# Joint attention of a diffusion transformer block: text scores, image gate rows and text V in one 32-column run behind the image scores

## The chip, the cores and the metric

One core of a Trainium2 chip runs the whole kernel in one launch. The metric is device time in microseconds (us) of that core; lower is better. TensorE does the matrix products, VectorE and ScalarE work on what it leaves in PSUM, GpSimd (POOL in the profile) and SyncE (SP) mostly issue transfers.

## The reference

Two streams, image (256 tokens) and text (32 tokens), batch 2, width 1152, all in bfloat16, are modulated, attend jointly and are projected out. With `_layernorm` and `_silu` as usual:

```python
mod_i = (_silu(c) @ wmod_img).reshape(B, 6, 1, D)      # shift, scale, gate: the first three are used
mod_t = (_silu(c) @ wmod_txt).reshape(B, 6, 1, D)
hi = _layernorm(x_img) * (1 + sci) + shi;  ht = _layernorm(x_txt) * (1 + sct) + sht
qkvi = hi @ wqkv_img;  qkvt = ht @ wqkv_txt             # q, k, v of each stream
q, k, v = concat([text, image], axis=1) of each
p = softmax(q @ k.T * D ** -0.5);  a = p @ v
out_i = x_img + gai * (ai @ wo_img);  out_t = x_txt + gat * (at @ wo_txt)
```

## The kernel before

All weights are streamed once through five weight slots of 128 x 9 x 1152; SP's queue issues these loads in program order, and a load into a used slot waits for the last reader of that slot. Instructions wrapped in `pin` keep their program order on their engine. What concerns the change is the stage between the last text projection (`qk_txt(1, w_k_t)`) and the output projections (`out_img`, L680).

**Scores.** For each of four image query tiles I0 to I3 (batch b, tile qi), `scores_img` (L584) makes 128 x 288 scores in PSUM with nine matmuls. `scores_txt` (L592) makes the scores of the 2 x 32 text queries with 18 matmuls in four 32-column groups of the array (`tile_position=(0, r0)`): even and odd feature tiles go to different halves, so the two halves must be added afterwards (`half`, a ScalarE copy at L657 and a VectorE add at L660).

**Softmax.** `soft_max` (L563, row maximum, VectorE), `soft_exp` (L570, exponential with row sum, ScalarE), `soft_div` (L575: reciprocal and multiplication on VectorE, and at L580 a small GpSimd multiplication which writes the 32 text-key columns a second time, to columns 320 to 351 of the row block `pb`, where the third key block is transposed from).

**Gate rows.** `img_gate` calls `mod_rows` (L509): 36 matmuls in four 32-column groups give the image gate's rows; a ScalarE copy (L516) takes them to SBUF, two GpSimd DMAs (L518) write them to DRAM. `img_gate_spread` (L528) reads them back over all 128 partitions as `gb`, which `out_img` multiplies by (L693).

**Text V.** `v_txt(r)` (L490) makes one half of the text values: 9 x 2 matmuls, each with both batches' 64 text tokens as 64 columns, in two column groups. `v_txt_out` subtracts a correction on VectorE.

**Transposes.** `p_transposes(b)` (L603) turns the softmax rows of image b by TensorE: 9 transposes of 128 x 128, three key blocks (`kj`) of three row tiles each, the third row tile being the text's `pbs["t"]`. Only `kj == 2` reads the columns that GpSimd wrote. ScalarE copies them to `pT` (L615), and `attn_pair` (L634) multiplies `pT` by the values.

In this stage TensorE's order is: I0, I1, text scores, gate rows, I2, I3, transposes of batch 0 (nine), text V (both halves), transposes of batch 1 (nine), attention. PSUM tiles come from two rings, `ps_mm` with six buffers and `ps_tr` with two. The GpSimd queue's order in this stage is: `pb` of I0, I1, the two gate-row DMAs, `pb` of the text, of I2, of I3, then the `gb` and `xf` loads.

Of the kernel before, what the change touches and what calls it, by code (L numbers as in the profile page):

```python
# [14 lines left out]
def kernel(  # L15
# [14 lines left out]
    nc = tc.nc  # L30
    bf = mybir.dt.bfloat16
    f32 = mybir.dt.float32
    PSUM = bass.MemoryType.PSUM

    B, NI, D = x_img.shape
    NT = x_txt.shape[1]
    P = 128
    KT = D // P
    NTOK = NI + NT
    NIT = (B * NI) // P  # L40
    TPB = NI // P
    NTT = B * NT
    CH = 384
    NCH = D // CH
    VC = 288
# [7 lines left out]
    work = ctx.enter_context(tc.tile_pool(name="work", bufs=2))  # L53
    small = ctx.enter_context(tc.tile_pool(name="small", bufs=4))
    ps_mm = ctx.enter_context(tc.tile_pool(name="ps_mm", bufs=6, space=PSUM))
    ps_tr = ctx.enter_context(tc.tile_pool(name="ps_tr", bufs=2, space=PSUM))

    pin = tc.keep_in_program_order

    def mm(*a, **k):  # L60
        return pin(nc.tensor.matmul(*a, **k))  # L61

    def tr(*a, **k):
        return pin(nc.tensor.transpose(*a, **k))  # L64
# [19 lines left out]
    def load_w(slot, src, c0, splits=(D,)):  # L84
        t = wtile(slot)
        sv = wview(src, c0)
        o = 0
        for n in splits:
            nc.sync.dma_start(t[:, :, o:o + n], sv[:, :, o:o + n])
            o += n  # L90
        return t
# [36 lines left out]
    ident = const.tile([P, P], bf)  # L128
# [22 lines left out]
    ident2 = const.tile([P, P], bf)  # L151
# [227 lines left out]
    HD = D // 2  # L379
# [3 lines left out]
    rows, cols = {}, {}  # L383
# [13 lines left out]
    hT_t = act.tile([P, KT, NTT], bf)  # L397
# [92 lines left out]
    def v_txt(r):  # L490
        ps = ps_mm.tile([P, VC], f32, tag="mm")
        for kt in range(KT):
            for g in range(2):
                c0 = g * HD + r * VC
                mm(ps[64 * g:64 * g + NTT, :], lhsT=hT_t[:, kt, :], rhs=w_v_t[:, kt, c0:c0 + VC],
                   start=(kt == 0), stop=(kt == KT - 1), tile_position=(0, 64 * g))
        return ps

    def v_txt_out(r, ps):
        pin(nc.vector.tensor_sub(v_t[:, r * VC:(r + 1) * VC], ps[:], svb[:, r * VC:(r + 1) * VC]))  # L500
        if r == 0:
            pin(nc.vector.tensor_sub(v_t[0:NTT, HD:HD + NTT], ps[NTT:P, 0:NTT], svb[NTT:P, 0:NTT]))
# [3 lines left out]
        r0 = 64 * h + NT * b  # L506
        return r0, v_t[r0:r0 + NT, c0:c0 + P]

    def mod_rows(w_blk, si):  # L509
        gps = ps_mm.tile([P, VC], f32, tag="mm")  # L510
        for kt in range(KT):
            for g in range(NGG):
                mm(gps[32 * g:32 * g + 32, :], lhsT=sT32[:, kt, :], rhs=w_blk[:, kt, g * VC:(g + 1) * VC],
                   start=(kt == 0), stop=(kt == KT - 1), tile_position=(0, 32 * g))
        g_sb = work.tile([P, VC], bf, tag="garow")
        pin(nc.scalar.copy(g_sb[:], gps[:]))  # L516
        for b in range(B):
            nc.gpsimd.dma_start(gsc[si, b, :].rearrange("(g j) -> g j", g=NGG), g_sb[b:P:32, :])  # L518
# [3 lines left out]
    xf = act.tile([P, 2, VC], bf)  # L522

    def img_gate():
        mod_rows(w_ga_i, 0)

    def img_gate_spread():
        for b in range(B):  # L528
            pin(nc.gpsimd.dma_start(gb[:, b, :], gsc[0, b, :].partition_broadcast(P)))
        for g in range(2):  # L530
            pin(nc.gpsimd.dma_start(xf[64 * g:64 * g + NTT, :, :],
                                    xt_flat.rearrange("t (r g j) -> g t r j", r=2, g=2)[g]))

    def txt_gate():
        mod_rows(w_ga_t, 1)
        for g in range(2):
            for b in range(B):
                r0 = 64 * g + 32 * b
                nc.gpsimd.dma_start(gbf[r0:r0 + NT, :, :],
                                    gsc[1, b, :].rearrange("(r g j) -> g r j", r=2, g=2)[g].partition_broadcast(NT))  # L540
# [4 lines left out]
    w_ga_i = load_w(0, wmod_img, 2 * D)  # L545
    w_v_t = load_w(1, wqkv_txt, 2 * D)
    w_o_i = load_rows(4, wo_img, 0)
    w_ga_t = load_w(3, wmod_txt, 2 * D)
# [8 lines left out]
    qpos = [[0, P, 2 * P], [NT, NT + P, 0]]  # L557

    pbs = {}
# [3 lines left out]
    def soft_max(key, sps, qn):  # L563
        nmx = small.tile([P, 1], f32, tag="nmx")
        pin(nc.vector.reduce_max(nmx[0:qn, :], sps[0:qn, :], axis=AX.X, negate=True))  # L565
        e = work.tile([P, NTOK], f32, tag="e")
        rs = small.tile([P, 1], f32, tag="rs")
        soft[key] = (sps, qn, nmx, e, rs)

    def soft_exp(key):  # L570
        sps, qn, nmx, e, rs = soft[key]
        pin(nc.scalar.activation(e[0:qn, :], sps[0:qn, :], ACT.Exp, bias=nmx[0:qn, :], scale=1.0,
                                 accum_out=rs[0:qn, :]))

    def soft_div(key):  # L575
        sps, qn, nmx, e, rs = soft[key]
        pin(nc.vector.reciprocal(rs[0:qn, :], rs[0:qn, :]))  # L577
        pb = pb_txt if key == "t" else pb_tiles[key[0] * TPB + key[1]]
        pin(nc.vector.tensor_scalar_mul(pb[0:qn, 0:NTOK], e[0:qn, :], rs[0:qn, :]))
        pin(nc.gpsimd.tensor_scalar(pb[0:qn, NI + 2 * NT:NI + 3 * NT], e[0:qn, NI:NTOK], rs[0:qn, :], 0.0,  # L580
                                     op0=ALU.mult, op1=ALU.add))
        pbs[key] = pb

    def scores_img(b, qi):  # L584
        q0 = qi * P
        sps = ps_mm.tile([P, NTOK], f32, tag="mm")
        for ft in range(KT):
            mm(sps[:], lhsT=qkT[:, ft, b, q0:q0 + P], rhs=qkT[:, KT + ft, b, :],
               start=(ft == 0), stop=(ft == KT - 1))
        return sps  # L590

    def scores_txt():  # L592
        sps = ps_mm.tile([P, NTOK], f32, tag="mm")
        for ft in range(KT):
            for b in range(B):
                r0 = 64 * (ft % 2) + NT * b
                mm(sps[r0:r0 + NT, :], lhsT=qkT[:, ft, b, NI:NTOK], rhs=qkT[:, KT + ft, b, :],
                   start=(ft < 2), stop=(ft >= KT - 2), tile_position=(0, r0))
        return sps

    pTs = {}

    def p_transposes(b):  # L603
        pT = work.tile([P, 3, NTOK], bf, tag="pT")
        tiles = [(range(3), ps_tr)] if b == 0 else [((2,), ps_mm), (range(2), ps_tr)]
        for kjs, pool in tiles:
            pT_ps = pool.tile([P, 8 * P], bf, tag="tr" if pool is ps_tr else "mm", name="pT_ps")
            txt = [(2, pbs["t"], ident2 if b else ident)]
            img = [(qi, pbs[(b, qi)], ident) for qi in range(TPB)]
            for n, kj in enumerate(kjs):  # L610
                for qi, pb, perm in (txt + img if b else img + txt):
                    o = n * NTOK + qpos[b][qi]
                    k0 = kj * P - (NT * b if kj == 2 else 0)
                    tr(pT_ps[:, o:o + P], pb[:, k0:k0 + P], perm[:])
            pin(nc.scalar.copy(pT[:, kjs[0]:kjs[-1] + 1, :],  # L615
                               pT_ps[:, 0:len(kjs) * NTOK].rearrange("p (k n) -> p k n", n=NTOK)))
        pTs[b] = pT

    def attn_keys(tiles, first):
        for b, dt in tiles:  # L620
# [25 lines left out]

    I = [(b, qi) for b in range(B) for qi in range(TPB)]

    sp = {key: scores_img(*key) for key in I[:2]}
    soft_max(I[0], sp[I[0]], P)  # L650
    soft_exp(I[0])
    soft_max(I[1], sp[I[1]], P)
    soft_div(I[0])
    soft_exp(I[1])
    st = scores_txt()
    half = work.tile([NTT, NTOK], f32, tag="half", bufs=1)
    pin(nc.scalar.copy(half[:], st[NTT:P, :]))  # L657
    soft_div(I[1])
    img_gate()
    pin(nc.vector.tensor_add(half[:], st[0:NTT, :], half[:]))  # L660
    soft_max("t", half, NTT)
    soft_exp("t")
    for key in I[2:]:
        sp[key] = scores_img(*key)
    soft_max(I[2], sp[I[2]], P)
    soft_exp(I[2])
    soft_div("t")
    soft_max(I[3], sp[I[3]], P)
    soft_exp(I[3])
    soft_div(I[2])  # L670
    soft_div(I[3])
    p_transposes(0)
    for r in range(2):
        v_txt_out(r, v_txt(r))
    p_transposes(1)
    img_gate_spread()
    for dts in ((0, 5, 1), (6, 2, 7), (3, 8, 4)):
        attn_pair(*[[(b, dt) for dt in dts] for b in range(B)])
# [37 lines left out]
    C3 = (CH, CH, CH)  # L716
    out_img(0, C3)
    out_img(1, C3, between=txt_gate)
    out_img(2, C3)
    out_txt()  # L720
# [31 lines left out]
```

## Time and profile before

| | us |
|---|---|
| median of 4 runs | 118.58 (117.89 to 118.74) |
| the profiled execution, its own time | 118.32 |
| its span, first to last instruction | 116.1 |
| TensorE busy in the span | 111.3 (96%), 1036 matmuls |
| VectorE / ScalarE / GpSimd busy | 72.0 / 44.9 / 12.4 |
| granted TensorE clock | 1.00 of full speed |
| DMA | 41.02 MB, mean 353 GB/s |

In the views of the profile an entry names the source line, the engine and the tiles: `sps` are scores, `gps` gate rows, `ps` here text V, `pT_ps` transposes, `aps` attention. All matmuls carry L61 and all transposes L64, the lines of two helpers. A timeline entry gives the start, the time to the end of the last instruction of the entry, and, in square brackets, the idle time before it with what ended it. Successive matmuls overlap, so their pace is read from starts, not from durations.

### The profile page before, as it was taken

To read this page: it belongs to the slowest core of one execution; us is meant where nothing else is said; L and a number is where in the kernel's file an instruction comes from. 1 tells how busy PE (TensorE), PEld (TensorE's weight loads), DVE (VectorE), ACT (ScalarE), POOL (GpSimd) and SP (SyncE) were. 2 spreads that over 40 slices of the span, in tenths; PEclk is the share of its full clock that TensorE was granted. 3 is DMA by queue.
4 is the path that set the end of the run, shared out by engine and by line. 5 is a ranking of instruction groups with operands and counts; after the bars stand their busy time and mean duration, and the time that the engine had idled before them with its cause. 6 is when DMAs were issued, how large, how long until landed. Compare 5 with 4: busy or idle time off the path is not lost.

```text
span 116.1 us, 2500 instructions
## 1 busy us (share of the span) xinstructions
PE 111.3 (96%) x1036; PEld 63.6 (55%) x1036; DVE 72.0 (62%) x151; ACT 44.9 (39%) x93; POOL 12.4 (11%) x34
## 2 busy tenths in 40 slices
PE   4999999999999999999999999999999999999990
PEld 2246544445584444445454458877866565557660
DVE  3478594063869999999996040017848566357671
ACT  5699610042652299825241223246747400100000
POOL 7300000000000000000000000004617000452000
PEclk9999999999999999999999999999999999999999
DMA  3999999999999999999999999999999999832223
GB/s 98 378 385 398 399 406 411 407 416 409 408 404 409 336 402 410 405 412 411 412 361 410 410 414 414 403 415 402 414 399 410 419 380 398 331 123 51 107 51 102
DMA packets 18917, 41.02 MB, mean 353 GB/s; under 512 B 1195, under 2 KB 1851, under 8 KB 18907
## 3 DMA queue, kind: packets, MB, share of 16 engines
q1 hardware_dynamic: 18032, 39.86, 89.1%
q0 software_dynamic: 480, 0.89, 2.2%
q10 hardware_dynamic: 395, 0.12, 0.4%
q8 instruction: 8, 0.13, 0.4%
q14 instruction: 2, 0.02, 0.0%
HBM read 39.52 MB, written 1.34 MB: 352 GB/s over the span
## 4 chain that ended last, share of the span: by engine, by line
PE 95%; DVE 2%; issue 0%; DVEq 0%
PE ps L61 53%; PE vps L61 15%; PE wps L61 7%; PE gps L61 5%; PE aps L61 5%; PE sps L61 5%; PE tp L64 2%; PE sc_ps L61 2%; PE pT_ps L64 1%; DVE tmp L693 1%; DVE o L694 0%; DVE warm L123 0%; PE tpt L64 0%; DVE hS_i L264 0%; DVE scc L257 0%
## 5 line engine op out<-in xcount | busy, mean ns | idle before, releaser
L61 PE MATMUL ps<-xT_i,t 128*128 128x512 bf16 x162 | 35.7, 379 | 0.0
L61 PEld LDWEIGHTS <-t 128*128 128x128 bf16 x324 | 20.4, 98 | 18.9 <-issue 0.5
L435 DVE SCALAR_TENSOR_TENSOR acc_sh<-t,sTf,acc_sh 128x1152 f32<-128x1152 bf16 x16 | 21.4, 1408 | 0.0
L61 PE MATMUL ps<-t,aT 128*128 128x384 bf16 (+3 forms) x153 | 20.3, 308 | 0.0
L61 PE MATMUL vps<-t,hS_i 128*128 128x512 bf16 (+1 forms) x108 | 17.9, 326 | 0.1
L61 PEld LDWEIGHTS <-aT 128*128 128x128 bf16 (+1 forms) x153 | 12.9, 101 | 7.2 <-issue 0.8
L61 PEld LDWEIGHTS <-hS_i 128*128 128x128 bf16 x108 | 9.0, 98 | 8.7 <-DVE hS_i L264 0.4
L365 ACT CAST qkT<-ps 128x512 bf16<-128x512 f32 (+2 forms) x11 | 6.1, 552 | 14.8 <-PE ps L61 13.5
L693 DVE TENSOR_TENSOR tmp<-ps,gb 128x384 bf16<-128x384 f32 (+2 forms) x13 | 6.8, 526 | 7.9 <-PE ps L61 7.9
L61 PE MATMUL wps<-warm 128*128 128x512 bf16 x25 | 8.7, 511 | 1.5 <-DVE unit L127 1.5
L580 POOL TENSOR_SCALAR pb<-e,rs 128x32 bf16<-128x32 f32 (+1 forms) x5 | 2.1, 417 | 74.4 <-DVE rs L577 74.4
L363 ACT ACTIVATE qkT<-ps 128x512 bf16<-128x512 f32 (+2 forms) x11 | 6.1, 561 | 8.4 <-PE ps L61 6.7
L180 DVE CAST v_i<-vps 128x512 bf16<-128x512 f32 x5 | 3.5, 692 | 7.5 <-PE vps L61 7.5
L565 DVE TENSOR_REDUCE nmx<-sps 128x1 f32<-128x288 f32 x4 | 1.8, 457 | 9.7 <-PE sps L61 9.7
L182 ACT CAST v_i<-vps 128x512 bf16<-128x512 f32 x4 | 2.3, 580 | 9.9 <-PE vps L61 9.9
L61 PEld LDWEIGHTS <-warm 128*128 128x128 bf16 x25 | 2.8, 122 | 5.7 <-issue 3.3
L61 PEld LDWEIGHTS <-sT 128*32 128x32 bf16 x180 | 4.6, 96 | 2.3 <-issue 1.6
L629 DVE TENSOR_SCALAR aT<-aps,svc 128x288 bf16<-128x288 f32 x9 | 4.3, 518 | 2.1 <-PE aps L61 2.1
L61 PE MATMUL sps<-qkT 128*128 128x288 bf16 (+1 forms) x54 | 5.5, 287 | 0.0
L61 PE MATMUL gps<-t,sT 128*32 128x288 bf16 x144 | 5.2, 287 | 0.0
L61 PE MATMUL aps<-pT,v_i 128*128 128x288 bf16 x36 | 5.1, 287 | 0.0
L61 PE MATMUL ps<-hT_t,t 128*128 128x64 bf16 x162 | 5.1, 193 | 0.0
(110 smaller groups left out, 105.4 us busy)
## 6 DMA issues: line engine op xcount, KB each, us to landing
t<-in_wqkv_txt_dram SPq DMA_DIRECT2D x3, 2592.0 KB, 18.9
t<-in_wmod_img_dram SPq DMA_DIRECT2D x2, 2592.0 KB, 14.1
t<-in_wmod_txt_dram SPq DMA_DIRECT2D x2, 2592.0 KB, 19.3
t<-in_wqkv_img_dram SPq DMA_DIRECT2D x3, 864.0 KB, 14.0
t<-in_wqkv_img_dram SPq DMA_DIRECT2D x1, 2592.0 KB
t<-in_wo_img_dram SPq DMA_DIRECT2D x3, 864.0 KB, 9.7
t<-in_wqkv_img_dram SPq DMA_DIRECT2D x3, 576.0 KB, 10.1
t<-in_wmod_txt_dram SPq DMA_DIRECT2D x2, 864.0 KB, 13.2
```

Of the source, the lines that this page charges most:

```text
L61: return pin(nc.tensor.matmul(*a, **k))
L64: return pin(nc.tensor.transpose(*a, **k))
L180: nc.vector.tensor_copy(out_ap, in_ap)
L182: nc.scalar.copy(out_ap, in_ap)
L363: nc.scalar.mul(out_ap, in_ap, SCALE)
L365: nc.scalar.copy(out_ap, in_ap)
L435: pin(nc.vector.scalar_tensor_tensor(acc, w_sh_t[:, kt, :], col, acc, op0=ALU.mult, op1=ALU.add))
L565: pin(nc.vector.reduce_max(nmx[0:qn, :], sps[0:qn, :], axis=AX.X, negate=True))
L580: pin(nc.gpsimd.tensor_scalar(pb[0:qn, NI + 2 * NT:NI + 3 * NT], e[0:qn, NI:NTOK], rs[0:qn, :], 0.0, op0=ALU.mult, op1=ALU.add))
L629: nc.vector.tensor_scalar(dst, tiles[(b, dt)][:], bias, None, op0=ALU.add)
L693: nc.vector.tensor_mul(tmp[:, 0:n], ps[:, 0:n], gb[:, b, c0:c0 + n])
```

## The change

All four image scores run first; then the text scores, the image gate rows and both halves of text V follow each other, all in four 32-column groups; then all 18 transposes run side by side. Text V's 64-column matmuls become twice as many 32-column ones, one for each batch. `p_transposes` is called by key block, with the copies of key blocks 0 and 1 on ScalarE and those of block 2 on VectorE. The ScalarE copy and the two DMAs of the gate rows (`gate_row`) are now put behind the text's exponential. In the built program the GpSimd queue holds `pb` of I0, I1, I2, I3, then the two gate-row DMAs, then `pb` of the text. On ScalarE the order is exponentials of I0, I1, I2, the `half` copy, exponentials of I3 and of the text, the gate-row copy, and two copies of `pT`.

```diff
 def v_txt(r):
             for g in range(2):
-                c0 = g * HD + r * VC
-                mm(ps[64 * g:64 * g + NTT, :], lhsT=hT_t[:, kt, :], rhs=w_v_t[:, kt, c0:c0 + VC],
-                   start=(kt == 0), stop=(kt == KT - 1), tile_position=(0, 64 * g))
+                for b in range(B):
+                    c0, r0 = g * HD + r * VC, 64 * g + NT * b
+                    mm(ps[r0:r0 + NT, :], lhsT=hT_t[:, kt, NT * b:NT * b + NT], rhs=w_v_t[:, kt, c0:c0 + VC],
+                       start=(kt == 0), stop=(kt == KT - 1), tile_position=(0, r0))
...
     def img_gate():
-        mod_rows(w_ga_i, 0)
+        rows["gi"] = mod_rows(w_ga_i)
+
+    def gate_row():
+        mod_row_out(rows["gi"], 0)
...
-    def p_transposes(b):
+    def p_transposes(b, kjs, pool, copy):
...
-            pin(nc.scalar.copy(pT[:, kjs[0]:kjs[-1] + 1, :],
-                               pT_ps[:, 0:len(kjs) * NTOK].rearrange("p (k n) -> p k n", n=NTOK)))
+        pin(copy(pTs[b][:, kjs[0]:kjs[-1] + 1, :],
+                 pT_ps[:, 0:len(kjs) * NTOK].rearrange("p (k n) -> p k n", n=NTOK)))
...
-    sp = {key: scores_img(*key) for key in I[:2]}
+    sp = {key: scores_img(*key) for key in I}
+    st = scores_txt()
+    img_gate()
+    vt = [v_txt(0)]
+    half = work.tile([NTT, NTOK], f32, tag="half", bufs=1)
     soft_max(I[0], sp[I[0]], P)
     soft_exp(I[0])
     soft_max(I[1], sp[I[1]], P)
     soft_div(I[0])
     soft_exp(I[1])
-    st = scores_txt()
-    half = work.tile([NTT, NTOK], f32, tag="half", bufs=1)
+    soft_max(I[2], sp[I[2]], P)
+    soft_div(I[1])
+    soft_exp(I[2])
+    soft_max(I[3], sp[I[3]], P)
+    soft_div(I[2])
     pin(nc.scalar.copy(half[:], st[NTT:P, :]))
-    soft_div(I[1])
-    img_gate()
+    soft_exp(I[3])
     pin(nc.vector.tensor_add(half[:], st[0:NTT, :], half[:]))
     soft_max("t", half, NTT)
+    soft_div(I[3])
     soft_exp("t")
-    for key in I[2:]:
-        sp[key] = scores_img(*key)
-    soft_max(I[2], sp[I[2]], P)
-    soft_exp(I[2])
+    gate_row()
     soft_div("t")
-    soft_max(I[3], sp[I[3]], P)
-    soft_exp(I[3])
-    soft_div(I[2])
-    soft_div(I[3])
-    p_transposes(0)
-    for r in range(2):
-        v_txt_out(r, v_txt(r))
-    p_transposes(1)
+    v_txt_out(0, vt[0])
+    vt.append(v_txt(1))
+    p_transposes(0, (0, 1), ps_tr, nc.scalar.copy)
+    v_txt_out(1, vt[1])
+    p_transposes(0, (2,), ps_mm, nc.vector.tensor_copy)
+    p_transposes(1, (2,), ps_mm, nc.vector.tensor_copy)
+    p_transposes(1, (0, 1), ps_tr, nc.scalar.copy)
     img_gate_spread()
```

More of the change, by code (lines that the diff above doesn't have):

```diff
@@ L507, in v_txt_cols, with mod_rows @@
         return r0, v_t[r0:r0 + NT, c0:c0 + P]
-    def mod_rows(w_blk, si):
+    def mod_rows(w_blk):
         gps = ps_mm.tile([P, VC], f32, tag="mm")
@@ L514, in mod_rows, with mod_row_out @@
                    start=(kt == 0), stop=(kt == KT - 1), tile_position=(0, 32 * g))
+        return gps
+    def mod_row_out(gps, si):
         g_sb = work.tile([P, VC], bf, tag="garow")
@@ L534, in txt_gate @@
     def txt_gate():
-        mod_rows(w_ga_t, 1)
+        mod_row_out(mod_rows(w_ga_t), 1)
         for g in range(2):
@@ L601 @@
     pTs = {}
-    def p_transposes(b):
[L604 to L614, printed above, removed]
-            pin(nc.scalar.copy(pT[:, kjs[0]:kjs[-1] + 1, :],
-                               pT_ps[:, 0:len(kjs) * NTOK].rearrange("p (k n) -> p k n", n=NTOK)))
-        pTs[b] = pT
+    def p_transposes(b, kjs, pool, copy):
+        pT_ps = pool.tile([P, 8 * P], bf, tag="tr" if pool is ps_tr else "mm", name="pT_ps")
+        txt = [(2, pbs["t"], ident2 if b else ident)]
+        img = [(qi, pbs[(b, qi)], ident) for qi in range(TPB)]
+        for n, kj in enumerate(kjs):
+            for qi, pb, perm in (txt + img if b else img + txt):
+                o = n * NTOK + qpos[b][qi]
+                k0 = kj * P - (NT * b if kj == 2 else 0)
+                tr(pT_ps[:, o:o + P], pb[:, k0:k0 + P], perm[:])
+        if b not in pTs:
+            pTs[b] = work.tile([P, 3, NTOK], bf, tag="pT", name="pT")
+        pin(copy(pTs[b][:, kjs[0]:kjs[-1] + 1, :],
+                 pT_ps[:, 0:len(kjs) * NTOK].rearrange("p (k n) -> p k n", n=NTOK)))
     def attn_keys(tiles, first):
```

## The prediction

> **What bounds the kernel now.** I read the page's chain first, to see which engine sets the end.
>
> ```profile
> ## 4 chain that ended last, share of the span: by engine, by line
> PE 95%; DVE 2%; issue 0%; DVEq 0%
> ```
>
> TensorE is on the chain from 14 us to 112 us without a gap, so a saving counts only if it shortens TensorE's queue, and any new gap there is paid in full. Next I read TensorE's timeline of the stage, for starts: the pace and the cost of passing from one kind of matmul to another.
>
> ```profile
> 75.90 3.09 PE L61 MATMUL sps<-qkT 128*128 128x288 bf16 x36
> 78.70 1.38 PE L61 MATMUL gps<-t,sT 128*32 128x288 bf16 x36
> 80.02 2.38 PE L61 MATMUL sps<-qkT 128*128 128x288 bf16 x18
> 82.23 0.67 PE L64 MATMUL pT_ps<-ident,pb 128*128 128x128 bf16 x9
> 82.83 2.40 PE L61 MATMUL ps<-t,hT_t 128*64 128x288 bf16 x36
> 85.16 0.68 PE L64 MATMUL pT_ps<-ident,pb 128*128 128x128 bf16 x9
> 85.67 0.90 PE L61 MATMUL aps<-pT,v_i 128*128 128x288 bf16 x6
> ```
>
> From 80.02 to 82.23 are 18 full-width matmuls: 0.123 us each. I0 and I1 (18 of the first entry's 36) thus end their turn at 75.90 + 2.21 = 78.11. Until 80.02, 1.91 us, come 54 matmuls in four groups. Four together at the pace of one make 13.5 rounds, 1.66 us; the remaining 0.25 is going into and out of this mode and the half-filled round. Nine transposes followed by attention take 85.67 - 85.16 = 0.51, those before text V 0.60: 0.09 is going in. Text V takes 2.33 for 18 rounds of two (2.21): 0.12 is going out. So one passage there and back costs 0.21 to 0.25.
>
> Then the engines that feed the transposes: the text softmax and the gate rows, on ScalarE, on VectorE and on GpSimd.
>
> ```profile
> 79.19 0.19 ACT L572 ACTIVATION_READ_ACCUMULATOR e<-sps,nmx 128x1 f32 x1
> 79.41 0.40 ACT L657 COPY half<-sps 64x288 f32<-64x288 f32 x1
> 80.15 0.40 ACT L516 CAST g_sb<-gps 128x288 bf16<-128x288 f32 x1 [0.34 <-PE gps L61]
> 80.92 0.53 ACT L572 ACTIVATE e<-half,nmx 64x288 f32<-64x288 f32 x1 [0.38 <-DVE nmx L565]
> 81.36 0.18 ACT L572 ACTIVATION_READ_ACCUMULATOR e<-half,nmx 64x1 f32 x1
> ```
>
> ```profile
> 79.91 0.44 DVE L660 TENSOR_TENSOR half<-sps,half 64x288 f32<-64x288 f32 x1
> 80.38 0.45 DVE L565 TENSOR_REDUCE nmx<-half 64x1 f32<-64x288 f32 x1
> 81.71 0.14 DVE L577 RECIPROCAL rs<-rs 64x1 f32<-64x1 f32 x1
> 93.12 0.56 DVE L693 TENSOR_TENSOR tmp<-ps,gb 128x384 bf16<-128x384 f32 x1 [0.94 <-PE ps L61]
> ```
>
> ```profile
> 80.84 1.33 POOL L518 DMA_DIRECT2D mod_scratch<-g_sb  x2 [0.70 <-ACT g_sb L516]
> 82.21 0.30 POOL L580 TENSOR_SCALAR pb<-e,rs 64x32 bf16<-64x32 f32 x1
> 86.75 1.17 POOL L529 DMA_DIRECT2D gb<-mod_scratch  x2 [2.41 <-DMA mod_scratch<-g_sb]
> ```
>
> The telling entry is the second of GpSimd's. The text's reciprocal ended at 81.85, but GpSimd's text columns began at 82.21, right behind the two gate-row DMAs (80.84 + 1.33 = 82.17): the issue of a DMA pair holds the queue for 1.33 us. It cost nothing, because the ninth transpose, the first to read these columns, started near 82.68 and they were ready at 82.51: a cover of 0.17.
>
> **The change, part by part.** *TensorE's work.* The scores and gate rows keep their number. Text V goes from 36 matmuls in two groups to 72 in four, 18 rounds both ways: 2.21. The 126 matmuls of the run make 31.5 rounds, half a round left as before. One passage there and back is gone, text V's own: -0.21. In the profile's time: image scores until 75.90 + 36 x 0.123 = 80.32, first text score at 80.41, transposes from 80.32 + 0.25 + 3.87 = 84.44, and without a wait attention at 84.44 + 2 x 0.51 = 85.46.
>
> A rule of the Trainium skill speaks against the finer tiling. The row first: text scores and gate rows ran 54 matmuls in 1.91 us, 35 ns each with both passages. "TensorE: Matmul & The Clock Gate" (section on 56 against 53.3 ns) says that with hardware decode off the sequencer spends about 62 ns on each matmul, which would make text V 72 x 62 ns = 4.5 us. The row denies that here, and I take the row.
>
> *The text softmax moves to the end.* Its scores' last matmul starts at 80.41 + 4 x 0.123 = 80.90 and lasts 0.29: 81.19. From there I use the steps of the same operations before. `half` copy 0.07 after TensorE's end (the gate copy's distance: 80.15 less 80.08): 81.26, with 0.40 to 81.66. Add 0.04 later: 81.70. Maximum +0.47 (79.91 to 80.38): 82.17. Exponential +0.54 (80.38 to 80.92): 82.71. Its sum is read at +0.44: 83.15. The gate-row copy stands behind it on ScalarE although its matmuls end near 82.3: +0.22 (79.19 to 79.41), 83.37, with 0.40 to 83.77. GpSimd's two DMAs +0.29 (80.55 to 80.84): 84.06. The text's columns, behind them, +1.37 (80.84 to 82.21): 85.43, with 0.30 to 85.73. TensorE goes on about 0.05 after (in the chain, the first image V matmul starts at 14.32, the VectorE scaling it waits for ended at 14.27): 85.78.
>
> *The new wait.* The ninth transpose is again the first that needs those columns (text rows, key block 2, batch 0); its place in the queue is 84.44 + 8 x 0.057 = 84.89. So TensorE stands for 85.78 - 84.89 = 0.89. Behind it in the queue are nine more transposes and all of attention. Sum: 0.89 - 0.21 = +0.68. The bounds: a copy behind an accumulator read has also come 0.09 after it (83.39 to 83.48), the later DMA pair at 99.42 took 1.19, which gives +0.41; a GpSimd operation of 0.47, as the 128-row ones have, gives +0.85. I take +0.68, since its rows are the same operations in the same stage.
>
> *Costed at nothing.* I3's exponential stands behind the `half` copy (from 81.6), its row block is ready at 83.3 on both engines; the first transpose of it has its place after 84.9. Text V reads its weights from 82.07 instead of 82.83; their load was issued at 61.48 and that group's median to landing is 18.9, so 80.4. The PSUM buffers that text V and two of the transpose tiles take over from the scores are read out by 82.2. The four `pT` copies: ScalarE's first is done long before attention; VectorE's two of 128x288 have no row here, between 0.40 (ScalarE's) and 0.69 (VectorE's 128x512): key block 2 of batch 1 would be ready by 87.5 at worst, while its first reader comes at attention + 0.84, 87.19 with the wait. With 0.45 each it is ready at 86.9, so I count nothing; at worst 0.3. ScalarE's last copy (0.64) ends near 87.2, its reader comes at 87.5. The text projection's weight load, which waits for text V, starts 0.7 earlier; nobody reads it before 105.
>
> *The gate itself.* Its write is issued 84.06 - 80.84 = 3.2 later, so the `gb` load goes out at about 89.97 and lands 5.5 to 6.1 after (its own rows): 95.5 to 96.1. VectorE wants it at 93.12 + 0.68 = 93.8 and waits about 2. TensorE does not: with six PSUM buffers the tile that needs the first output tile's buffer back, the seventh, starts near 100.8, and VectorE, 0.95 per tile against TensorE's 1.46, catches up. The store of the first image tile leaves 2 us later, far from the end.
> "DMA: Bandwidth & Descriptors" (anatomy of a DMA issued from GpSimd) puts such a DMA at 2.0 us plus its bytes over 436 GB/s; by that `gb` would land before 90.5 and VectorE never wait. The trace has 5.5 us, and I keep it; the sum is the same.
>
> **The sum.** The profiled execution took 118.32, 0.26 below the median of the runs. 118.32 + 0.68 = 119.00; against the median, 119.26, or 0.6% more. What a measurement of this kernel can tell from no change is about 0.5%, 0.59 us.
>
> **Rivals.** *The wait does not come* (not slower). GpSimd's text columns are done before 84.85, 0.9 earlier than I have them; this would need the DMAs not to hold the queue, and the entries at 80.84 and 82.21 speak against it. Then only -0.21 is left: 118.11, by the median 118.37, within 0.5%. Chance 0.10.
> *The gate comes too late.* If `gb` lands after 100.8 instead of 96, TensorE runs out of PSUM buffers and every further microsecond is paid: at 102, +0.68 + 1.2 = +1.9, 120.5. For it: transfers still fill the DMA engines until 100. Against: a margin of nearly 5. Chance 0.04.
> *Text V does not run four wide.* At the present 62 to 65 ns per matmul (2.33 over 36), 72 take 2.2 to 2.3 more; the wait is then covered, and +2.25 - 0.21 gives +2.0, 120.6. Against it: the gate rows. Chance 0.06.
>
> **How the numbers follow.** The forecast has 0.80, with its own range of 119.0 to 119.45 by the median. Two thirds of it lie over 0.59: 0.55 slower, 0.25 the same. With the late gate and slow text V, 0.10: slower 0.65. The first rival lies within the bound except for the scatter of the runs (0.85 from lowest to highest): 0.06 same, 0.04 faster. So faster 0.04, same 0.31, slower 0.65. The range takes in the first rival and, above, the 0.3 of the copies and scatter: 118.3 to 119.8; the two dear rivals, 0.10, stay out.
>
> **What would show it.** Right: in TensorE's timeline the transposes start near 84.4 and are torn once, by about 0.9, between the eighth and the ninth, with GpSimd's `pb` of the text as what ended the idle time; attention starts near 86.35. GpSimd's gate-row DMAs start near 84.1, its last `pb` near 85.4. Text V takes 4 rounds in 0.49. The first multiplication by `gb` starts near 95.5 without a gap on TensorE. Wrong: transposes in one piece, a start of attention before 85.6, or a gap elsewhere, above all ahead of text V or in the output projections.

## The result, and the profile after

The changed kernel takes 118.7 us (median of 54 runs, 117.86 to 119.35), the kernel before 118.3 (78 runs, 117.62 to 119.05). The ratio is 1.0031, 95% interval 1.0018 to 1.0044: slower by 0.37 us, clear of no change, but only a little over half of the 0.68 forecast and inside the 0.5% bound. The forecast's main case, slower by more than the bound, did not come; the mechanism did, with one term too large. (The bound itself was too wide for this many runs: the interval is 0.26% from end to end, and tells a change of 0.3% from none.)

TensorE's timeline of the stage after the change (start, length of the entry, idle time before it in brackets):

```profile
76.14 5.29 PE L61 MATMUL sps<-qkT 128*128 128x288 bf16 x54
81.15 1.38 PE L61 MATMUL gps<-t,sT 128*32 128x288 bf16 x36
82.25 2.49 PE L61 MATMUL ps<-t,hT_t 128*32 128x288 bf16 x72
84.67 0.62 PE L64 MATMUL pT_ps<-ident,pb 128*128 128x128 bf16 x8
85.86 0.73 PE L64 MATMUL pT_ps<-ident,pb 128*128 128x128 bf16 x10 [0.56 <-POOL pb L587]
86.42 0.90 PE L61 MATMUL aps<-pT,v_i 128*128 128x288 bf16 x6
```

The transposes are torn between the eighth and the ninth, and what ended the idle time is GpSimd's text columns. The eighth starts at 84.67 + 0.62 - 0.22 (its own length) = 85.07; the ninth, due 0.06 later, at 85.86. By starts the gap is 0.73; the 0.56 in brackets counts only from the modelled end of the eighth.

The chain that ended last now leaves TensorE in this stage. Its pieces in order of time (start, length, what):

```profile
76.30 5.15 PE sps L61 x54
81.45 0.02 issue
81.48 0.40 ACT half L669
81.88 0.02 issue
81.90 0.46 DVE half L671
82.36 0.02 issue
82.39 0.45 DVE nmx L572
82.83 0.08 DVE rs L584
82.91 0.01 issue
82.93 0.63 ACT e L579 x2
83.56 0.29 ACT g_sb L520
83.85 0.29 issue
84.14 0.73 POOL mod_scratch L522
84.86 0.00 issue
84.87 0.60 POOL mod_scratch L522
85.46 0.04 issue
85.50 0.31 POOL pb L587
85.81 0.05 issue
85.86 0.73 PE pT_ps L64 x10
```

Read downwards, it is the forecast's own chain: text scores, `half` copy and add, maximum, exponential, gate-row copy, two DMA issues, text columns, ninth transpose. (`DVE rs` between maximum and exponential is the reciprocal of I3, which the text's exponential does not read; the exponential starts 0.09 after the end of the maximum, as it did before: 82.84 to 82.93, and 80.83 to 80.92.) The text columns do not need the gate rows. They only stand behind them on GpSimd.

The two profiles' spans differ by 0.8 us (116.1 and 116.9), which is more than the change. Before the stage the program is the same, yet the first image score started at 75.90 in the one profile and at 76.14 in the other; over the eleven profiles of this study it started between 75.88 and 76.64. In nine of them the chain runs through the landing of the first modulation weights; the two without it, the kernel before and experiment 5, are the two earliest. So I compare the stage from the first image score to the first attention matmul. Before it was 85.67 - 75.90 = 9.77, after it is 86.42 - 76.14 = 10.28: +0.51, at the upper end of what the times allow (0.21 to 0.52). (These are differences of rounded starts; from unrounded ones the two are 9.78 and 10.29, as the expectations below have them.) What follows the first attention matmul is the same length in both.

### The profile page after: what moved, and what is told of

Its sections match the earlier page's. It is cut to its first block, busy times and chain, and to the rows that moved or that the text cites. A ratio compares the mean times of both kernels' runs of the same rounds, so it can differ in the third digit from the quotient of the medians.

```text
span 116.9 us, 2569 instructions
## 1 busy us (share of the span) xinstructions
PE 111.0 (95%) x1072; PEld 63.5 (54%) x1072; DVE 72.4 (62%) x153; ACT 44.0 (38%) x92; POOL 12.3 (11%) x34
## 4 chain that ended last, share of the span: by engine, by line
PE 82%; DMA 8%; DVE 2%; POOL 1%; ACT 1%; SPq 1%; issue 1%; DVEq 0%
PE ps L61 51%; PE vps L61 15%; DMA t<-in_wmod_img_dram 8%; PE aps L61 5%; PE sps L61 4%; PE gps L61 4%; POOL mod_scratch L522 1%; PE sc_ps L61 1%; SPq L104 1%; PE tp L64 1%; PE pT_ps L64 1%; DVE tmp L701 1%; ACT e L579 1%; DVE o L702 0%; DVE half L671 0%
```

## Experiments

Theory A: the two DMA issues in front of the text columns are the loss, and one passage between tilings less is a gain. Theory B: the text softmax, moved to the end, is too late by itself.

**1. Text columns first.**

```diff
-    gate_row()
     soft_div("t")
+    gate_row()
```

> The changed kernel with one order turned round: GpSimd multiplies the text's key columns first and issues the two gate-row DMAs after them. Stage length is counted from the first image score to the first attention matmul on TensorE: 9.78 us before, 10.29 in the changed kernel. Theory A (the two DMA issues in front of the text's columns are the new wait; one passage between tilings less is a small gain): the gap of 0.73 in the transposes goes, stage 9.56, time 0.2 us under before, ratio 0.998. Theory B (the text softmax itself is too late once it comes last, whatever GpSimd does first): the gap stays over 0.5, stage over 10.0, ratio over 1.002.

The ratio was 1.0007 (0.9986 to 1.0029). GpSimd's timeline, the chain at the start of attention, and TensorE's transposes:

```profile
84.34 0.46 POOL L587 TENSOR_SCALAR pb<-e,rs 64x32 bf16<-64x32 f32 x1 [0.37 <-DVE rs L584]
84.75 1.33 POOL L522 DMA_DIRECT2D mod_scratch<-g_sb  x2
```

```profile
85.25 0.46 PE pT_ps L64 x6
85.70 0.02 issue
85.72 0.65 ACT pT L621
86.37 0.04 issue
86.41 5.94 PE aps L61 x54
```

```profile
85.18 1.18 PE L64 MATMUL pT_ps<-ident,pb 128*128 128x128 bf16 x18
```

The text columns are done at 84.80, before the transposes begin at 85.18, and all eighteen transposes run in one piece. Theory B falls. But the stage is 86.41 - 76.64 = 9.77, that of the kernel before, and not 9.56: the gain of 0.21 is missing. The chain says where it is: attention now waits for ScalarE's copy of batch 0's first two key blocks. Of theory A the cause of the loss held; the gain it promised did not come.

**2. Gate-row copy ahead of the text's exponential.**

```diff
-    soft_exp("t")
     gate_row()
+    soft_exp("t")
     soft_div("t")
```

> The changed kernel with ScalarE's gate-row copy ahead of the text's exponential instead of behind it; GpSimd still issues the two DMAs before the text's columns. Theory A: the DMAs then start right behind GpSimd's columns of I3, near 83.5 in the changed profile's time instead of 84.14, the text's columns end near 85.2 instead of 85.8, the gap shrinks from 0.73 to about 0.1, stage 9.65, ratio about 0.999. Theory B: the text's exponential is if anything later by up to 0.1, so the gap stays or grows, ratio 1.003 to 1.005.

The ratio was 1.0008 (0.9984 to 1.0032). GpSimd, then TensorE and ScalarE:

```profile
83.26 0.47 POOL L587 TENSOR_SCALAR pb<-e,rs 128x32 bf16<-128x32 f32 x1 [1.15 <-DVE rs L584]
83.67 1.43 POOL L522 DMA_DIRECT2D mod_scratch<-g_sb  x2
85.14 0.30 POOL L587 TENSOR_SCALAR pb<-e,rs 64x32 bf16<-64x32 f32 x1
```

```profile
84.94 1.28 PE L64 MATMUL pT_ps<-ident,pb 128*128 128x128 bf16 x18
86.18 0.90 PE L61 MATMUL aps<-pT,v_i 128*128 128x288 bf16 x6
```

```profile
85.49 0.64 ACT L621 COPY pT<-pT_ps 128x576 bf16<-128x576 bf16 x1 [1.66 <-PE pT_ps L64]
```

The DMAs start right behind I3's columns, as expected, and the text columns end at 85.44 instead of 85.80, although the image scores here began 0.27 later. The tear in the transposes shrinks to 0.10: all eighteen take 1.28, against 1.18 in one piece. The stage is again 9.77 (76.41 to 86.18), not 9.65: the same copy (85.49 to 86.13) ends 0.05 before attention, about the distance of experiment 1. The chain of this profile does not name the copy, so here the reading rests on these times.

**3. Twice as many gate-row writes.** Each of the two writes is divided into two of half the columns:

```diff
-            nc.gpsimd.dma_start(gsc[si, b, :].rearrange("(g j) -> g j", g=NGG), g_sb[b:P:32, :])
+            for j in range(2 if si == 0 else 1):
+                w = VC // 2 if si == 0 else VC
+                nc.gpsimd.dma_start(gsc[si, b, :].rearrange("(g j) -> g j", g=NGG)[:, j * w:(j + 1) * w],
+                                    g_sb[b:P:32, j * w:(j + 1) * w])
```

> The changed kernel with the image gate's rows written by four DMAs of half the columns instead of two. Theory A: two issues held GpSimd for 1.33 us, four hold it for 2.5 to 2.7, so the gap in the transposes grows by 1.2 to 1.35 to about 2.0, stage 11.5 to 11.65, ratio to before 1.013 to 1.015. Theory B: the issues lie beside the wait, ratio stays at 1.003 to 1.005.

The ratio was 1.0125 (1.0103 to 1.0148), 1.5 us.

```profile
84.39 2.45 POOL L524 DMA_DIRECT2D mod_scratch<-g_sb  x4 [0.67 <-ACT g_sb L520]
86.88 0.30 POOL L590 TENSOR_SCALAR pb<-e,rs 64x32 bf16<-64x32 f32 x1
```

Four issues hold GpSimd for 2.45 instead of 1.33, and the stage grows from 10.28 to 87.80 - 76.39 = 11.41. The 1.12 of issue became 1.13 of stage: here every microsecond of DMA issue in front of the text columns is paid by TensorE. The bytes are the same, so it is not the bytes. The number of issues doubled, and with it the number of pieces of rows; that it is the issues and not the pieces is suggested, not shown, by the two `gb` loads, which go to 128 partitions with 288 KB each and held GpSimd for only 1.17 (the entry at 86.75 in the prediction). The growth is a little under my 1.2 to 1.35, because the two added issues took 0.56 each.

**4. Text V four wide, nothing else.** The kernel before with the new `v_txt` alone.

> The kernel before with text V alone in 32-column matmuls, at its old place between the two sets of transposes. Theory A: 18 rounds of four take what 18 rounds of two took, text V 2.33 us, stage 9.78, ratio 1.000 within 0.001. Rival: 72 matmuls cost their own issue time, 62 ns each, 2.2 us more, stage near 12.0, ratio 1.018.

The ratio was 1.0007 (0.999 to 1.0024). TensorE:

```profile
83.08 2.39 PE L61 MATMUL ps<-t,hT_t 128*32 128x288 bf16 x72
85.40 0.68 PE L64 MATMUL pT_ps<-ident,pb 128*128 128x128 bf16 x9
```

72 matmuls take 2.32 from start to start, 32 ns each, as 36 of double width did (2.33). The stage is 85.92 - 76.15 = 9.77. Four-wide text V is free, and gains nothing by itself.

Experiments 1 and 2 left a new question: is it the copy that keeps the 0.21? Theory A2 says yes, and that the gap hides it in the changed kernel; rival B2 says that the copy only ends at the same time.

**5. The first copy divided between two engines,** on top of experiment 1:

```diff
-    p_transposes(0, (0, 1), ps_tr, nc.scalar.copy)
+    p_transposes(0, (0,), ps_tr, nc.scalar.copy)
     v_txt_out(1, vt[1])
+    p_transposes(0, (1,), ps_mm, nc.vector.tensor_copy)
```

> The reordered kernel (text columns ahead of the gate-row DMAs) with batch 0's first copy divided: key block 0 on ScalarE as before, key block 1 on VectorE, from two PSUM tiles. Theory A2 (with the gap gone the start of attention waits for the one ScalarE copy of both key blocks, 0.65 us, 0.28 more than the last transpose allows): half the copy is done by the end of the transposes, attention follows the eighteenth transpose at once, stage 9.55 instead of 9.77, ratio to before 0.998. Rival B2 (the transposes themselves or the softmax hold attention, the copy only ends at the same time): stage stays at 9.7 to 9.8, ratio 1.000.

The ratio was 0.9981 (0.9962 to 1.0001). TensorE, ScalarE, VectorE:

```profile
84.41 1.18 PE L64 MATMUL pT_ps<-ident,pb 128*128 128x128 bf16 x18
85.42 0.90 PE L61 MATMUL aps<-pT,v_i 128*128 128x288 bf16 x6
```

```profile
84.79 0.40 ACT L621 COPY pT<-pT_ps 128x288 bf16<-128x288 bf16 x1 [1.22 <-PE pT_ps L64]
```

```profile
84.95 0.74 DVE L621 COPY pT<-pT_ps 128x288 bf16<-128x288 bf16 x3
```

Key block 0 is copied by 85.19, key block 1 (the first of VectorE's three) by about 85.25, and attention follows the eighteenth transpose at 85.42. The stage, begun at 75.88, is 9.55, 0.23 under before (both from unrounded starts). This is the passage that the reordering saves, for once kept to the end. The division does two things at once: the first copy can start after three transposes instead of six, and two engines share the work. No run separates them.

**6. The divided copy with GpSimd's order as in the changed kernel.**

> The changed kernel with the same divided copy, but with GpSimd's order as in the changed kernel (gate-row DMAs first). Theory A2: the gap of 0.73 in the transposes covers the copy anyway, stage 10.29, ratio 1.003 to 1.004. Rival B2: if the copy had a share in the loss of the changed kernel, stage falls to 10.0 or 10.1.

The ratio was 1.0039 (1.0016 to 1.0062), the stage 86.63 - 76.35 = 10.28, that of the changed kernel. As A2 had it: while the gap is there, the copy costs nothing and dividing it gains nothing.

**7. All copies on ScalarE,** on top of experiment 1 (the two `nc.vector.tensor_copy` become `nc.scalar.copy`).

> The reordered kernel with all four copies of the transposes on ScalarE, as in the kernel before: undoes the part of the change that gave key block 2 to VectorE. Theory A2: attention starts as late as in the reordered kernel (stage 9.77), since the first copy is the same; ScalarE's fourth copy ends about 0.5 us later (two copies of 0.34 in front of it), so batch 1's keys wait 0.1 to 0.2 us in attention, ratio 1.002. Rival: the copies on VectorE change nothing, attention takes 5.77 us as in all kernels.

The ratio was 0.9999 (0.9971 to 1.0028), and the rival was right: attention took its usual 5.77.

```profile
85.22 1.79 ACT L621 COPY pT<-pT_ps 128x576 bf16<-128x576 bf16 x4 [1.38 <-PE pT_ps L64]
```

```profile
87.08 1.64 PE L61 MATMUL aps<-pT,v_i 128*128 128x288 bf16 x12
```

All four copies end at 87.01, just in time: the last one holds batch 1's key blocks 0 and 1, and these are first read at 87.08. Giving key block 2 to VectorE, which is part of the change, is worth nothing in this order.

**8. Text V 64 columns wide again,** on top of experiment 1.

> The reordered kernel with text V in 64-column matmuls again, directly behind the 32-column gate rows. Theory A: a passage from one column width to another costs as much as one between tiled and full width, 0.1 us; the transposes start 0.1 later, and with them the copy and attention, stage 9.87, ratio 1.001. Rival (only the way between full width and tiles costs; or the half-filled round is closed by it): 0 to 0.06 more, stage 9.77 to 9.83.

The ratio was 1.001 (0.9984 to 1.0036).

```profile
81.38 1.39 PE L61 MATMUL gps<-t,sT 128*32 128x288 bf16 x36
82.70 2.40 PE L61 MATMUL ps<-t,hT_t 128*64 128x288 bf16 x36
85.03 1.18 PE L64 MATMUL pT_ps<-ident,pb 128*128 128x128 bf16 x18
```

From gate rows to text V it is 1.32, against 1.10 where both are 32 wide (81.15 to 82.25 above): 0.22 more. From text V to the transposes it is 2.33 (82.70 to 85.03), against 2.42 (82.25 to 84.67): 0.09 less, presumably because the half-filled round no longer stands at the end of the run. That leaves 0.12 to 0.13, and by as much the stage is over experiment 1: 86.27 - 76.37 = 9.90 from the rounded starts, 9.89 from the unrounded. So in this run going from one column width to another cost like going from tiles to the full array, about 0.1, as theory A had it; the time alone could not tell the two theories apart. The finer tiling thus has a use: not its pace, but that it keeps the run in one mode.

**9. Experiment 5 again,** for the interval.

> The reordered kernel with the divided copy once more, for a narrower interval. Its stage was 9.55 us against 9.78 before, so 0.23 us or 0.19% is expected: ratio 0.998, and the interval of both sets together should leave out 1.000. Rival: the stage's gain does not reach the end, ratio 1.000.

The ratio was 0.9975 (0.9949 to 1.0002), the stage again 85.96 - 76.41 = 9.55. Each interval takes in 1; weighted by their widths the two give 0.998, 0.996 to 0.9995, which leaves it out. It is the fastest of the kernels here, about a quarter of a microsecond under the kernel before.

## Why the prediction was right in its mechanism and wrong in its size

**TensorE's work: right.** The transposes were due 84.44 - 75.90 = 8.54 after the first image score and came at 84.67 - 76.14 = 8.53. One passage there and back less was put at -0.21; it measured -0.23 where nothing hides it (experiment 5). Four-wide text V costs nothing, experiment 4.

**The chain of the text softmax: right up to the gate-row copy.** Counted from the first image score, `half` copy, maximum and exponential were forecast at 5.36, 6.27 and 6.81; they came at 5.34, 6.25 and 6.79.

**The step that failed: the gate-row copy behind the exponential, a term that was too large.** I took +0.22 from the start of the accumulator read, as before the `half` copy, and 0.40 for the copy. ScalarE:

```profile
83.37 0.19 ACT L579 ACTIVATION_READ_ACCUMULATOR e<-half,nmx 64x1 f32 x1
83.46 0.38 ACT L520 CAST g_sb<-gps 128x288 bf16<-128x288 f32 x1
```

It was +0.09 and 0.38, so the DMAs started 0.16 sooner in the stage than forecast (8.00 instead of 8.16). Everything behind kept its distance: 1.36 to the text columns against 1.37, 0.36 from there to TensorE against 0.35. So the gap was 0.73 instead of 0.89, and the sum 0.73 - 0.21 = +0.52 against a measured +0.51. The distance of 0.09 stood in the prediction, as the lower bound from a copy with the same neighbour; I preferred the row of the same stage. It was not scatter: the `half` copy kept 0.22 in both profiles where it follows the read (before and experiment 4), and the gate-row copy 0.09 to 0.10 in every profile that has it behind the text's exponential. Why the `half` copy kept more, no run shows.

**What followed from this.** The bound was 0.59; +0.68 lay over it by 0.09, less than this one term was wrong, so with the term right the sum would have stayed inside. Of the prediction's own bounds, +0.41 to +0.85, the stage's +0.51 keeps both, and the +0.37 of the times lies just under the lower. Of the 0.31 between +0.68 and the measured +0.37 the shorter gap is 0.16, nearly all of it this term. Most of the rest, 0.14, lies between the stage of one profile (+0.51) and the medians of the times; the interval just allows it (up to 0.52), experiment 6 has the same stage and a ratio of 1.0039, and no run explains it further. The absolute number missed another 0.3, because the four runs shown had a median of 118.58 where 78 have 118.3.

**The first rival was priced wrongly.** Without the gap I expected -0.21. Experiment 1, and experiment 2 with a tear of only 0.10, gave a stage as long as before: "ScalarE's first is done long before attention" was true only with the wait in place. With the gap gone, the copy of 576 columns on one engine takes 0.71 from the end of the sixth transpose to attention (85.70 to 86.41 in experiment 1), while the eighteenth would have let attention go at 85.18 + 1.01 = 86.19: 0.22 lost, just what the passage had saved. Experiment 1 takes GpSimd off TensorE's path altogether, so no order on GpSimd alone could have made the reordering faster; it needed the divided copy as well.

**The other rivals stayed out.** Text V ran four wide (experiment 4). The gate did come late, and it was hidden:

```profile
89.96 1.17 POOL L536 DMA_DIRECT2D gb<-mod_scratch  x2 [4.16 <-PE aps L61]
```

```profile
96.27 0.56 DVE L701 TENSOR_TENSOR tmp<-ps,gb 128x384 bf16<-128x384 f32 x1 [3.35 <-DMA gb<-mod_scratch]
```

The `gb` load was issued at 89.96 (forecast 89.97). That agreement may be partly luck: the forecast counts from the landing of the rows' write, while the profile names an attention matmul as what ended GpSimd's wait. The load landed 6.2 to 7.2 after its issue instead of 5.5 to 6.1, VectorE began to multiply 3.15 later than before (93.12), and TensorE did not notice: from its first output matmul (91.45 before, 92.20 after) to the end of its last piece in the chain (112.45, 113.20) it took 21.0 us in both.

## What to carry to other kernels

When a step is moved, follow its DMA issues into the queue that they pass, and ask who stands behind them there: two issues of 0.6 to 0.7 us on GpSimd held a 0.3 us multiplication, and with it TensorE, though the data had nothing to do with each other. Removing a gap uncovers what it hid, so price the case without the wait from the copies and loads as they then stand. And where two rows give one step different lengths, as 0.09 and 0.22 here, and the sum lies near the bound of what can be measured, carry both through to the answer: nothing in the profile before said which of them would hold.

## What the runs showed of the hardware that was not expected

A passage between two column widths (32 to 64) cost about as much as one between tiles and the full array: 0.12 us in the one profile that has it (experiment 8), against 0.09 to 0.12 read from the kernel before. VectorE's copies of 128x288 bfloat16 from PSUM lasted 0.30 us (the changed kernel and experiment 5), ScalarE's of the same shape 0.40. And with the same program ahead of it, the stage began anywhere between 75.88 and 76.64 us in eleven profiles, a scatter larger than every effect studied here except that of the four writes.
